# An mLSTM and two expert stages in one kernel: one transfer for q and k, three more staging buffers, all products of w3 first, the causal mask by TensorE

## The chip, the cores and the metric

The kernel runs on one core of one Trainium2 chip. Time is device time in microseconds (us). Each kernel is executed several times and once more under the hardware profiler; the profiled execution gives the trace from which all rows here are taken.

## What is computed

```python
for t in range(S):                                   # mLSTM, B=4, H=8, S=768, D=40
    m_new = maximum(f[t] + m, i[t])
    C = exp(f[t] + m - m_new) * C + exp(i[t] - m_new) * outer(v[t], k[t])
    n = exp(f[t] + m - m_new) * n + exp(i[t] - m_new) * k[t]
    y[t] = sigmoid(o[t]) * (C @ q[t]) / maximum(abs(n . q[t]), 1.0)
    m = m_new
x = y as [3072 tokens, 320]
x = ((x @ w1) * (x @ w2)) @ w3 @ w_out               # stage A, width 1024
out = maximum(x @ u1, x @ u2, x @ u3) @ u_out        # stage C, width 768
```

The weights come as 64-bit floats, all else as 32-bit floats; the output is 32-bit.

## The kernel before, in words

**Units.** The mLSTM is done in chunks of L = 87 time steps of one batch row, for all 8 heads at once: 4 x 9 = 36 units. `prepare` loads a unit's q and k (tile raw, two transfers, one for each half of the heads), q again at the partitions of the state (qq) and k and v (kv). `decay` makes the factors between time steps (tile dd). For the first 9 units (`ND`) it does so with a product on TensorE (L597) followed by exp on ScalarE (L600); later units load the exponents from a table d_na in DRAM, which four writes (L458) put there. In both cases GpSimd then zeroes what lies above the diagonal (`affine_select`, L615). `visit(v)` runs the score products of unit v (L675) and the output and state products of unit v-1 (L684). `rest` carries the state over (L720), divides (L732 to L735), multiplies by the gate (L740, GpSimd) and copies 64 columns to the tile's end (L743, GpSimd). `turn_x` transposes y (L750); `x_parts` splits it into a rounded part xh and its remainder xl.

**Blocks.** The two expert stages run over 8 blocks of 384 tokens. An A step (`a_step`) makes 128 columns of x @ w1 and x @ w2, in 16 products of 384 columns (L789 to L794); a `b_step` multiplies their product by w3 @ w_out (L899 to L903). `c_step` and `d_step` (L918) do the same for stage C. The order is A0 A1 C0 C1 A2 A3 and so on; visits stand at fixed steps (`USTEPS`), and from step `RIDE` on a visit is put into the middle of a step, where it can carry along the transposes of the unit before.

**Weights.** `granule` loads 512 columns of 64-bit weights (512 KB) into a staging buffer and turns them into 32-bit floats in place or into a target: ScalarE (L987), a shift on VectorE (L996) or its equal on ScalarE (L993), and VectorE (L1004). `parts` and `rem` split the result (L1014, L1017, L1029, L1036). There are three staging buffers stg and one, sx, that is there until the stage C weights come. `fold(ft)` decodes two granules of w3 and multiplies them with w_out at full 32-bit precision (L1054), as w3 @ w_out is needed once: 8 folds, five in the visits 1 to 5 (`FOLDS`), three ahead of the `b_step` that needs them. The first fold also decodes the 5 granules of w_out.

**Order.** No instruction order is written by hand. Each operation is entered with its engine, an assumed duration and the tiles that it reads and writes; `Plan.run` gives each a latest start, adds a correction from the table `BIAS`, and simulates the engines, always issuing the ready operation of the lowest value. An operation with two engines goes to the one that is free. All loads and stores are issued from one queue, SP's. A tile of a ring waits for the tile that had the buffer before.

**Shared space.** The tiles y, og, ev and pr lie in one buffer, misc, over the tiles of the gate computation (ff, aug, gft and others). A gate operation holds each ring back until the gate tiles below it have been read, the four writes of L458 among the readers of gft. A tile "kv" has the unit's data in partitions 0 to 95 and an identity matrix (`eyes`) in partitions 87 to 126, loaded once for each of its 3 buffers (L513).

Of the kernel before, what the change touches and what calls it, by code (L numbers as in the profile page):

```python
# [8 lines left out]
F32 = mybir.dt.float32  # L9
# [13 lines left out]
TB = 384  # L23
NBLK = B * S // TB
# [6 lines left out]
PRE = 6  # L31
# [26 lines left out]
XT_NS = 200  # L58
BIAS = {
# [3 lines left out]
    "Awa": 1483620, "Awar": 210300, "Awb0": -305840, "Awb1": 295600, "Awc": 213380, "Awcr": 343750, "Awd": 126180,  # L63
# [14 lines left out]
    "Gqqb": 186930, "Gwa": -943910, "Gwar": 1016950, "Gwc": 269610, "Gwcr": 31530, "Gwd": 243890, "Gy0": -450790,  # L78
# [26 lines left out]
def pool(n):  # L105
    return 150 + 2.1 * n


class Plan:
# [11 lines left out]
    def op(self, eng, ns, fn, r=(), w=(), after=(), cols=0, port=0, early=None):  # L121
# [163 lines left out]
def mlstm_moe_kernel(  # L285
# [50 lines left out]
    made["one", 0] = y[:, NCH * L + 1:NCH * L + 33]  # L336
    slots_nm = [lw["r", 0].rearrange("p a b c -> p (a b c)")[:, 0:8 * LE],
# [3 lines left out]
    for pool_, tag, bufs, n in (  # L341
# [3 lines left out]
        (tmp, "sx", EX, 1024), (tmp, "w3", L_BUFS, 512), (tmp, "raw0", RAW0, 8 * L),  # L345
# [8 lines left out]
    shared = (("y", TB), ("og", DM), ("ev", TB), ("pr", TB))  # L354
# [138 lines left out]
    P.op("G", 900, lambda: G.tensor_copy(na()[2][64:96], na()[1]), r=[("g", "msk")], w=[("hl", 1, 0)])  # L493
# [6 lines left out]
    new(("pt", 0), [128, NCH, 32], F32, "ac2")  # L500
# [11 lines left out]
    for i, t in enumerate(slots["kv"]):  # L512
        dma(71, lambda t=t: SP.dma_start(out=view(t, [128, 8, 81], F32)[L:R, :, 0:40], in_=eyes), w=[("kvb", i)])  # L513
# [4 lines left out]
    for c in range(SIGN):  # L518
        dma(318, lambda c=c: SP.dma_start(out=sg0[0:LP, c], in_=og[0, c]), w=[("sg", (0, c))])
# [57 lines left out]
    def decay(q):  # L577
# [5 lines left out]
        if q < ND:  # L583
# [9 lines left out]
            P.op(("V", "G"), (dve(8 * LE), 1400), (lambda: masked(V), lambda: masked(G)), r=[("hl", 1), ("one", 0)],  # L593
                 w=[("nm", q)], port=1)
# [673 lines left out]
```

## Time and profile before

| | us |
|---|---|
| median of 3 runs | 684.59 (682.53 to 685.3) |
| the profiled execution, its own time | 684.24 |
| its span, first to last instruction | 682.5 |
| TensorE busy in the span | 651.5 (95%) |
| VectorE, ScalarE, GpSimd busy | 372.9, 289.3, 248.0 |

PE is TensorE, PEld its weight loads, DVE VectorE, ACT ScalarE, POOL GpSimd, SPq the queue from which transfers are issued. L and a number is a line of the kernel. The time outside the span, 684.24 - 682.5 = 1.74 us, is launch and end.

### The profile page before, as it was taken

How to read it: one execution, taken by the hardware profiler on the slowest of the kernel's cores; microseconds unless marked ns; L12 is line 12 of the kernel's file. 1: busy time of each engine (PE TensorE's matmuls, PEld its weight loads, DVE VectorE, ACT ScalarE, POOL GpSimd, SP SyncE). 2: the span in 40 equal slices, each digit the busy share in tenths (PEclk: the TensorE clock that was granted, in tenths of full speed). 3: DMA queues.
4: the chain of work that ended last, by engine and by line, in shares of the span. 5: the costliest groups of instructions: out<-in, count | busy, mean ns of one | idle time of the engine just before them, and what ended most of it. 6: DMA issues, size and time to landing. Idle time of an engine off the chain costs nothing.

```text
span 682.5 us, 15124 instructions
## 1 busy us (share of the span) xinstructions
PE 651.5 (95%) x6199; PEld 618.1 (91%) x6199; DVE 372.9 (55%) x709; ACT 289.3 (42%) x546; POOL 248.0 (36%) x251
## 2 busy tenths in 40 slices
PE   3689989999999999999999999999999999999997
PEld 2456889899999999999999999999999989999997
DVE  7949985888853375443444474534344463323332
ACT  5726977656822435352522435432422322323111
POOL 4818972954521365232332354232132320000000
PEclk9999999999999999999999999999999999999999
DMA  8978769545520254211223162222023100000000
GB/s 211 265 219 248 229 190 273 167 131 165 162 80 30 64 158 127 65 48 29 61 69 79 48 175 75 68 69 67 2 78 82 40 30 1 1 1 1 1 30 29
DMA packets 33331, 65.97 MB, mean 97 GB/s; under 512 B 8974, under 2 KB 15502, under 8 KB 33262
## 3 DMA queue, kind: packets, MB, share of 16 engines
q1 hardware_dynamic: 33262, 65.01, 33.7%
q8 instruction: 48, 0.79, 0.5%
q14 instruction: 21, 0.17, 0.1%
HBM read 60.96 MB, written 4.03 MB: 95 GB/s over the span
## 4 chain that ended last, share of the span: by engine, by line
PE 84%; DVE 7%; ACT 3%; DMA 3%; issue 2%; POOL 1%; SPq 1%; DVEq 0%; POOLq 0%; ACTq 0%
PE wk L789 13%; PE wk L790 13%; PE wk L791 13%; PE acs L918 9%; PE wk L792 7%; PE wk L794 5%; PE acs L899 5%; PE acs L903 4%; PE wk L1054 3%; PE aq L684 3%; PE acs L901 3%; PE aq L675 2%; PE wk L804 1%; PE wk L750 1%; DVE w L1004 1%
## 5 line engine op out<-in xcount | busy, mean ns | idle before, releaser
L816 ACT CAST ph<-misc 128x384 fp32r<-128x384 f32 (+1 forms) x114 | 57.7, 507 | 144.7 <-PE acs L918 59.3
L866 DVE TENSOR_TENSOR misc<-misc,wk 128x384 f32<-128x384 f32 (+1 forms) x98 | 53.2, 545 | 113.9 <-PE wk L794 91.0
L642 POOL TENSOR_TENSOR pk<-qq,dd 63x696 f32<-63x696 f32 (+1 forms) x30 | 50.4, 1681 | 133.4 <-issue 117.6
L789 PE MATMUL wk<-xh,wch 128*128 128x384 f32 x288 | 97.1, 337 | 0.9 <-DVE misc L837 0.9
L791 PE MATMUL wk<-xl,wch 128*128 128x384 f32 x288 | 96.9, 337 | 0.0
L790 PE MATMUL wk<-xh,wcl 128*128 128x384 f32 x288 | 96.9, 336 | 0.0
L820 DVE TENSOR_TENSOR pl<-misc,ph 128x384 fp32r<-128x384 f32 (+1 forms) x91 | 60.5, 666 | 52.2 <-ACT ph L816 51.5
L789 PE MATMUL wk<-xh,wah 128*128 128x384 f32 x256 | 87.5, 342 | 0.0
L790 PE MATMUL wk<-xh,wal 128*128 128x384 f32 x256 | 86.3, 337 | 0.7 <-DVE wal L1017 0.7
L791 PE MATMUL wk<-xl,wah 128*128 128x384 f32 x256 | 86.1, 336 | 0.0
L837 DVE TENSOR_TENSOR misc<-misc,wk 128x384 f32<-128x384 f32 x64 | 35.1, 549 | 79.1 <-PE wk L794 46.4
L820 POOL TENSOR_TENSOR pl<-misc,ph 128x384 fp32r<-128x384 f32 (+1 forms) x23 | 24.5, 1067 | 146.6 <-ACT ph L816 108.6
L835 ACT COPY misc<-wk 128x384 f32<-128x384 f32 x64 | 30.5, 477 | 63.8 <-PE wk L804 35.2
L789 PEld LDWEIGHTS wk<-xh,wch 128*128 128x128 f32 x288 | 54.1, 188 | 1.2 <-DVE misc L837 1.2
L791 PEld LDWEIGHTS wk<-xl,wch 128*128 128x128 f32 x288 | 54.0, 188 | 0.0
L790 PEld LDWEIGHTS wk<-xh,wcl 128*128 128x128 f32 x288 | 54.0, 188 | 0.0
L608 POOL TENSOR_TENSOR dd<-am,dd 127x696 f32<-127x696 f32 (+2 forms) x27 | 39.0, 1448 | 38.0 <-DMA dd<-d_na 37.7
L918 PE MATMUL acs<-wd,ph 128*128 128x320 f32 x288 | 51.6, 313 | 0.7 <-DVE misc L961 0.7
L790 PEld LDWEIGHTS wk<-xh,wal 128*128 128x128 f32 x256 | 48.2, 188 | 1.5 <-DVE wal L1017 1.3
L789 PEld LDWEIGHTS wk<-xh,wah 128*128 128x128 f32 x256 | 48.2, 188 | 0.6 <-DVE xl L771 0.3
L792 PE MATMUL wk<-xh,wcr 128*128 128x384 f32 x144 | 48.4, 336 | 0.0
L791 PEld LDWEIGHTS wk<-xl,wah 128*128 128x128 f32 x256 | 48.2, 188 | 0.0
(144 smaller groups left out, 1351.9 us busy)
## 6 DMA issues: line engine op xcount, KB each, us to landing
raw<-in_qk SPq DMA_DIRECT2D x72, 130.5 KB, 4.0
kv<-in_kv SPq DMA_DIRECT2D x36, 243.0 KB, 3.5
dd<-d_na SPq DMA_DIRECT2D x21, 348.0 KB, 5.0
stg<-in_w3t SPq DMA_DIRECT2D x13, 512.0 KB, 6.3
stg<-in_wc SPq DMA_DIRECT2D x9, 512.0 KB, 4.4
qq<-in_qs SPq DMA_DIRECT2D x32, 130.5 KB, 4.0
out<-misc SPq DMA_DIRECT2D x24, 160.0 KB, 1.9
misc<-in_og SPq DMA_DIRECT2D x31, 120.0 KB, 3.3
```

The costliest lines, as they stand in the source:

```text
L608: P.op("G", 1400, lambda: G.tensor_tensor(out=T("dd", q)[:r], in0=am[:r, c, h0:h0 + 8].unsqueeze(2).to_broadcast([r, 8, n]), in1=T("dd", q ...
L642: e.tensor_tensor(out=T("pk", q)[64:R, :, 0:n], in0=T("qq", q)[64:R, :, 0:n], in1=T("dd", q)[64:R], op=ALU.mult)
L789: PE.matmul(p, lhsT=h_[:, kt], rhs=xh[:, kt], start=kt == 0, stop=False)
L790: PE.matmul(p, lhsT=l_[:, kt], rhs=xh[:, kt], start=False, stop=False)
L791: PE.matmul(p, lhsT=h_[:, kt], rhs=xl[:, kt], start=False, stop=False)
L792: PE.matmul(p, lhsT=r_, rhs=xh[:, 2], start=False, stop=False)
L794: PE.matmul(p, lhsT=r_, rhs=xl[:, 2], start=False, stop=True)
L816: P.op("A", act(n), lambda sl=sl: A.copy(out=T("ph", key)[:, sl], in_=T(*src)[:, sl]), r=[src + part], w=[("ph", key) + part])
L820: e.tensor_tensor(out=T("pl", key)[:, sl], in0=T(*src)[:, sl], in1=T("ph", key)[:, sl].bitcast(F32), op=ALU.subtract)
L837: P.op("V", dve(TB), lambda: V.tensor_tensor(out=T(*sa), in0=T(*sa), in1=T(*ps[1]), op=ALU.mult), r=[ps[1]], w=[sa])
L866: P.op("V", dve(sl.stop - sl.start), lambda sl=sl: V.tensor_tensor(out=T(*sc)[:, sl], in0=T(*sc)[:, sl], in1=T(*ps)[:, sl], op=ALU.max), r ...
L918: PE.matmul(T(f"ac{m}", (k, 1)), lhsT=src[:, m * 128:m * 128 + 128], rhs=w[:, o:o + DM], start=first_, stop=last_,)
```

## The change

- A unit's q and k come in one transfer of 112 partitions (rows 40 to 63 and 104 to 111 are padding) in place of two of 48.
- The buffer sx goes. Three buffers, s2, are laid over the place of ev and pr in misc, and used until the fourth A step of block 0 (`NP0` = 3); the first three A steps put their results into tiles of their own, pr0. The ring of staging buffers is 6 long until then and 3 long after, where it was 4 and later 3.
- All 8 folds stand in the visits 1 to 4.
- For the first 9 units the causal mask is added by TensorE: the product of an identity (eye) and a tile (tri) with 0 and -1e30 goes into PSUM ahead of the product of L597. GpSimd's `affine_select` stays for the other 27 units.
- `eyes` is loaded into partitions 96 to 127 alone, which the load of kv doesn't touch.
- The product of L635 and that of L740 may go to GpSimd or VectorE, the copy of L743 to ScalarE or GpSimd.
- Visits are placed at other steps (in blocks 2 to 7 one to two steps earlier), and at steps without a visit no unit is kept back for a ride: its transposes run there by themselves.
- The assumed durations and the table of corrections are new; the blocks' sizes and order are written in another way and stay the same (8 of 384, A0 A1 C0 C1 ...).

```diff
-FOLDS = (1, 2, 3, 4, 5)
+FOLDS = (1,1,1,2,2,3,3,4)
+NP0 = 3
-EX = 1
+EX = 0
...
+    made["eye", 0] = y[:, 1024:1152]
+    made["tri", 0] = x[:, NCH * 128:NCH * 128 + 4 * LE].rearrange("p (a b) -> p a b", b=LE)
...
-        (tmp, "sx", EX, 1024), (tmp, "w3", L_BUFS, 512), (tmp, "raw0", RAW0, 8 * L),
+        (tmp, "sx", EX, 1024), (tmp, "w3", L_BUFS, 512), (tmp, "raw0", RAW0, 8 * L), (tmp, "pr0", NP0, TB),
...
+    o = where["ev"][0]
+    slots["s2"] = [misc[:, o + i:o + i + 1024] for i in range(0, where["pr"][1] - o - 1023, 1024)]
+    where["s2"], over["s2"] = (o, where["pr"][1]), []
...
+    P.op("A", 300, f, r=[("cs", 0)], w=[("eye", 0)])
+    def f():
+        t = T("tri", 0).bitcast(F32)
+        G.memset(t, 0.0)
+        G.affine_select(out=T("tri", 0)[0:L], in_=t[0:L], pattern=[[0, 4], [1, LE]], compare_op=ALU.is_ge, fill=-1e30, base=0,
+                        channel_multiplier=-1)
...
-        dma(71, lambda t=t: SP.dma_start(out=view(t, [128, 8, 81], F32)[L:R, :, 0:40], in_=eyes), w=[("kvb", i)])
+        dma(71, lambda t=t: SP.dma_start(out=view(t, [128, 8, 81], F32)[LP:128, :, 0:40], in_=eyes), w=[("kvb", i)])
...
-                P.op("P", 190, lambda g=g, key=key: PE.matmul(
-                    T(*key), lhsT=T("hl", 0)[:, c], rhs=T("nm", q)[:, g * 4:g * 4 + 4], start=True, stop=True
-                ), cols=352, r=[("hl", 0), ("nm", q)], w=[key])
+                def f(g=g, key=key):
+                    PE.matmul(T(*key), lhsT=T("eye", 0), rhs=T("tri", 0), start=True, stop=False)
+                    PE.matmul(T(*key), lhsT=T("hl", 0)[:, c], rhs=T("nm", q)[:, g * 4:g * 4 + 4], start=False,
+                              stop=True)
+                P.op("P", 350, f, cols=704, r=[("hl", 0), ("nm", q), ("eye", 0), ("tri", 0)], w=[key])
...
-        for g in range(2):
-            dma(333, lambda g=g: SP.dma_start(out=T("raw", q)[g * 64:g * 64 + 48], in_=qk[b, c, g]), w=[("raw", q, g)])
+        dma(586, lambda: SP.dma_start(out=T("raw", q)[0:112], in_=qk[b, c]), w=[("raw", q)])
...
-        p = "sx" if not switch and i % (STG + EX) < EX else "stg"
+        ring = ["stg"] * STG + ["sx"] * (EX * (not switch)) + ["s2"] * (len(slots["s2"]) * (not s2_end))
+        p = ring[i % len(ring)]
...
+            if j == NP0:
+                s2_end.append(P.op("S", 0, lambda: None, after=[
+                    x for key, (_, _, acc) in P.state.items() if key[0] == "s2" for x in acc]))
+                gates_done["ev"] = gates_done["pr"] = s2_end[0]
...
-        keep = at >= RIDE and cur[0] <= NU and (kind == "C" or cols[0] >= (k + 1) * TB)
+        keep = at >= RIDE and cur[0] <= NU and at in visits and (kind == "C" or cols[0] >= OFF[k + 1])
```

## Rows read from the trace of the kernel before

**Rows 1.** Busy time of each engine in stretches of the span.

```profile
core 0: us, PE busy (x) PEld busy (x) DVE busy (x) ACT busy (x) POOL busy (x), PEclk, DMA share, GB/s
0.00:9.30 9.30, 0.00 (x0) 0.00 (x0) 6.32 (x7) 2.97 (x4) 4.42 (x14) 1.00 0.76 200
9.30:33.20 23.90, 15.36 (x197) 11.68 (x197) 21.62 (x30) 18.21 (x34) 15.91 (x13) 1.00 0.92 250
33.20:46.80 13.60, 12.35 (x37) 7.95 (x39) 5.91 (x15) 2.85 (x5) 4.14 (x5) 1.00 0.80 223
46.80:71.20 24.40, 21.88 (x383) 16.10 (x384) 22.16 (x43) 15.92 (x32) 17.87 (x16) 1.00 0.83 242
71.20:97.00 25.80, 23.00 (x326) 20.53 (x326) 23.10 (x41) 19.56 (x37) 21.04 (x19) 1.00 0.67 200
97.00:145.00 48.00, 48.00 (x324) 43.77 (x323) 35.99 (x55) 35.05 (x64) 29.26 (x25) 1.00 0.70 208
...
165.00:678.80 513.80, 511.81 (x4758) 499.71 (x4756) 238.86 (x494) 182.28 (x347) 143.28 (x151) 1.00 0.22 59
```

**Rows 2.** Timeline of PE: a fold half early and late, the first A group.

```profile
33.26 4.64 PE L1054 MATMUL wk<-wof,w 128*128 128x320 f32 x8 [0.66 <-DVE w L1004]
...
66.48 2.32 PE L1054 MATMUL wk<-wof,w 128*128 128x320 f32 x8
...
71.24 0.34 PE L789 MATMUL wk<-xh,wah 128*128 128x384 f32 x1
71.42 0.34 PE L790 MATMUL wk<-xh,wal 128*128 128x384 f32 x1
```

**Rows 3.** Timeline of PE at the sixth fold.

```profile
118.12 4.58 PE L1054 MATMUL wk<-wof,w 128*128 128x320 f32 x16
122.29 0.58 PE L789 MATMUL wk<-xh,wah 128*128 128x384 f32 x1
122.70 0.33 PE L790 MATMUL wk<-xh,wal 128*128 128x384 f32 x1
122.88 0.34 PE L791 MATMUL wk<-xl,wah 128*128 128x384 f32 x1
```

**Rows 4.** DMA from 0 to 71.2 us: packets, and the queue's share.

```profile
DMA packets 7538, 16.78 MB, mean 236 GB/s; under 512 B 2398, under 2 KB 3166, under 8 KB 7530
## 3 DMA queue, kind: packets, MB, share of 16 engines
q1 hardware_dynamic: 7530, 16.68, 83.7%
```

**Rows 5.** What SP's queue waited for, 20 to 71.2 us: total, times, longest.

```profile
SPq L982 <- DVE w L1004: 7.0, 4, 2.6
SPq L982 <- DVE wof L1004: 5.6, 4, 2.5
SPq L536 <- DMA kv<-in_eyes: 5.1, 1, 5.1
```

**Rows 6.** Timeline of SP's queue around the writes of d_na.

```profile
40.96 0.31 SPq L536 DMA_DIRECT2D kv<-in_kv  x1
41.32 0.42 SPq L625 DMA_DIRECT2D raw<-in_qk  x1
41.84 0.85 SPq L982 DMA_DIRECT2D stg<-in_w3t  x2
42.73 1.52 SPq L458 DMA_DIRECT2D d_na<-misc  x4
```

**Rows 7.** The page's DMA issues: KB each, median us from issue to landing.

```profile
raw<-in_qk SPq DMA_DIRECT2D x72, 130.5 KB, 4.0
kv<-in_kv SPq DMA_DIRECT2D x36, 243.0 KB, 3.5
dd<-d_na SPq DMA_DIRECT2D x21, 348.0 KB, 5.0
stg<-in_w3t SPq DMA_DIRECT2D x13, 512.0 KB, 6.3
```

**Rows 8.** Groups by line and shape, 0 to 97 us: busy us, mean ns.

```profile
L615 POOL TENSOR_SCALAR_AFFINE_SELECT dd<-dd 87x696 f32<-87x696 f32 x9 | 11.3, 1258 | 0.1
...
L1004 DVE SCALAR_TENSOR_TENSOR w<-stg 128x512 int32<-128x512 int32 x8 | 8.3, 1033 | 1.0 <-ACT stg L987 1.0
...
L597 PE MATMUL wk<-wcr,wch 128*128 128x352 f32 x10 | 5.0, 538 | 2.9 <-ACT dd L600 1.9 <-DVE wcr L587 1.0
...
L1065 DVE TENSOR_TENSOR wb<-wk,wb 128x256 fp32r<-128x256 f32 x5 | 2.1, 412 | 0.0
...
L996 DVE TENSOR_SCALAR stg<-stg 128x512 int32<-128x512 int32 x4 | 1.8, 443 | 4.5 <-DMA stg<-in_w3t 4.5
```

**Rows 9.** Timeline of PE: transposes in a ride and by themselves.

```profile
197.08 0.44 PE L750 MATMUL wk<-cs,misc 87*128 87x87 f32 x3
197.31 1.12 PE L918 MATMUL acs<-wd,ph 128*128 128x320 f32 x6
...
233.72 0.39 PE L750 MATMUL wk<-cs,misc 87*128 87x87 f32 x3
233.90 1.12 PE L918 MATMUL acs<-wd,ph 128*128 128x320 f32 x6
```

More of the change, by code (lines that the diff above doesn't have):

```diff
@@ L42 @@
 STG = 3
-EX = 1
+EX = 0
 L_BUFS = 4
 RCP = 8
-LAST = (NBLK - 1, 1, NC - 1)
 LATE = ("A", 1, 4)
 OC = 4 * L
+TB = max(SIZES)
+NBLK = len(SIZES)
+OFF = [sum(SIZES[:k_]) for k_ in range(NBLK + 1)]
+STEPS = [(x_[0], int(x_[1:]), j_) for x_ in ORDER.split() for j_ in range(8 if x_[0] == "A" else 6)]
+LAST = (NBLK - 1, 1, NC - 1)
+UNITS = [(t_ // S) * NCH + -(-(t_ % S) // L) for t_ in OFF[1:]]
+PRE = UNITS[0] + 1
 BUF = dict(x=3, y=3, og=3, ph=2, ev=3, raw=2, kv=3, qq=2, dd=3, pk=2)
@@ L166, in op @@
         name = tag + str(self.phase)
-        if self.phase == 0 and eng[0] in "DP":
+        if self.phase < 2:
             k = self.count[tag] = self.count.get(tag, -1) + 1
@@ L686, in f @@
             if turned:
-                turn_x(*turned)
+                turn_x(turned)
         r = [("raw", v)] * (v < NU) + [("pk", q), ("kv", q)] * (q >= 0)
         w, early, ns = list(toks), {}, 0
-        for has, part, cost in ((turned, None, XT_NS), (q >= 0, "o", 850), (v < NU, "s", 850), (pair, "p", 173)):
+        for has, part, cost in ((turned, None, XT_NS), (q >= 0, "o", 800), (v < NU, "s", 930), (pair, "p", 215)):
             if has:
@@ L765, in x_parts, with x_cols @@
+    def x_cols(key):
+        new(("xt", key), [128, 3, 128], F32, "wk")
+        P.op("P", 220, lambda: turn_x(key), cols=110, r=[("y", key[:2]), ("cs", 0)], w=[("xt", key)])
+        x_parts(key)
+    def x_parts(key):
+        b, c, t, end = key
+        t0 = b * S + c * L
+        cols[0] += end - t
+        while t < end:
+            k = max(x for x in range(NBLK) if OFF[x] <= t)
+            e = min(end, OFF[k + 1])
+            if t == OFF[k]:
                 xtiles((k, 0))
-            src = slice(t - c * L, e - c * L)
@@ L773, in x_parts @@
                 in1=T("xh", (k, 0))[:, :, to].bitcast(F32), op=ALU.subtract,
-            ), r=[("xt", (b, c)), ("xh", (k, 0), c)], w=[("xl", (k, 0), c)])
+            ), r=[("xt", key), ("xh", (k, 0), c)], w=[("xl", (k, 0), c)])
             t = e
-    def xtiles(key):
-        new(("xh", key), [128, 3, TB], F32R, "xh")
-        new(("xl", key), [128, 3, TB], F32R, "xl")
+    made_x = []
+    turns = [(0, 0), (1, 0)]
+    for k_ in range(NBLK):
+        turns += [(k_, 1), (k_ + 2, 0)]
+    turns = [x for x in turns if x[0] < NBLK]
@@ L782, in group @@
+    def xtiles(key):
+        while key not in made_x:
+            x = turns[len(made_x)]
+            made_x.append(x)
+            new(("xh", x), [128, 3, SIZES[x[0]]], F32R, "xh")
+            new(("xl", x), [128, 3, SIZES[x[0]]], F32R, "xl")
     def group(ps, key, wh, wl, wr, r, rest=True):
@@ L808, in thirds @@
     def thirds(key):
-        return [((m,), slice(m * 128, m * 128 + 128)) for m in range(3)] if key == LAST else [((), slice(0, TB))]
+        n = SIZES[key[0]]
+        return [((m,), slice(m * 128, m * 128 + 128)) for m in range(n // 128)] if key == LAST else [((), slice(0, n))]
     def phl(src, key):
-        new(("ph", key), [128, TB], F32R, "ph")
-        new(("pl", key), [128, TB], F32R, "pl")
+        n = SIZES[key[0]]
+        new(("ph", key), [128, n], F32R, "ph")
+        new(("pl", key), [128, n], F32R, "pl")
         for part, sl in thirds(key):
@@ L939, in split @@
         def split(kt, src, alt=False):
-            P.op("A", act(TB, not alt), lambda: A.copy(out=T("xh", key)[:, kt], in_=T(*src)),
+            P.op("A", act(n, not alt), lambda: A.copy(out=T("xh", key)[:, kt], in_=T(*src)),
                  r=[src], w=[("xh", key, kt)])
@@ L1013, in parts @@
         key, w = g
-        P.op("A", act(n), lambda: A.copy(out=h_(), in_=w()), r=[key], w=[tok + ("h",)], after=after)
+        P.op("A", wide(n), lambda: A.copy(out=h_(), in_=w()), r=[key], w=[tok + ("h",)], after=after)
         def f(e):
@@ L1108, in can, with some @@
     def can():
-        return pend and (pend[0][0] == 0 or ("xh", (0, 1)) in made)
+        if not pend:
+            return False
+        b, c, t, end = pend[0]
+        new_ = [(k, 0) for k, x in enumerate(OFF[:-1]) if t <= x < end and (k, 0) not in made_x]
+        i = len(made_x) - BUF["x"]
+        return not new_ or new_ == [turns[len(made_x)]] and (i < 0 or turns[i] in finished)
+    def some(k):
+        b, c, t, end = pend.pop(0)
+        x_cols((b, c, t, OFF[k + 1]))
+        pend.insert(0, (b, c, OFF[k + 1], end))
     def more(pair=None):
@@ L1126, in mlstm_moe_kernel @@
         while len(pend) > XLAG:
-            x_cols(*pend.pop(0))
+            x_cols(pend.pop(0))
     while pend:
-        x_cols(*pend.pop(0))
-    steps = []
-    for p in range(NBLK // 2):
-        for kind, nj in (("A", NA), ("C", NC)):
-            for k in (2 * p, 2 * p + 1):
-                steps += [(kind, k, j) for j in range(nj)]
-    nu = {}
-    for p in range(NBLK // 2):
-        span = [s for s in steps if s[1] // 2 == p]
-        for j in USTEPS:
-            nu[span[j]] = 1
+        x_cols(pend.pop(0))
+    at_a = [STEPS.index(("A", k, 0)) for k in range(NBLK)] + [len(STEPS)]
+    visits, v = {}, PRE
+    for k in range(1, NBLK):
+        a, n = at_a[k - 1], UNITS[k] + 1 - v
+        room = at_a[k] - a - VLAG[k > 1]
+        for i in range(n):
+            visits.setdefault(a + i * room // n, []).append(v + i)
+        v = UNITS[k] + 1
+    assert v == NU + 1 and all(len(x) == 1 for x in visits.values()), visits
+    finished = set()
     def last(src, key):
@@ L1159, in mlstm_moe_kernel @@
     gate = {}
-    for at, s in enumerate(steps):
+    for at, s in enumerate(STEPS):
         kind, k, j = s
@@ L1170, in mlstm_moe_kernel @@
             for q in range(3):
-                gate[q] = late_w(q) if q else [P.op("S", 0, lambda: None, w=[("hl", 0), ("hl", 1), ("one", 0)],
+                gate[q] = late_w(q) if q else [P.op("S", 0, lambda: None, w=[("hl", 0), ("hl", 1), ("one", 0), ("eye", 0), ("tri", 0)],
                                                          after=nm)]
@@ L1202, in _lay @@
     qs[:, :, 8:48] = qk[:, :, :, :, :, 0].transpose(0, 1, 3, 2, 4, 5)
-    rows = np.zeros((B, NCH, 2, 48, 4, 2 * L), f)
-    rows[:, :, :, 0:D] = qk.reshape(B, NCH, 2, D, 4, 2 * L)
+    rows = np.zeros((B, NCH, 112, 4, 2 * L), f)
+    for g in range(2):
+        rows[:, :, g * 64:g * 64 + D] = qk[:, :, g].reshape(B, NCH, D, 4, 2 * L)
     eye = np.eye(D, dtype=f)
@@ L1238, in _lay @@
         "kv": kvt,
[L1239 removed]
+        "eyes": np.repeat(np.concatenate([eye[LP - L:], eye[0:1] * 0])[:, None], H, 1),
         "og": og,
```

202 lines of the change are left out of this document (109 added, 93 removed), and 61 rows, old and new, of the table BIAS.

## The prediction

> **What bounds the kernel now.** I read the busy time by stretches first [rows 1]. From 97 us on TensorE has no gap to speak of: 48.0 of 48.0 us up to 145, and 511.8 of 513.8 from 165 to the last product. There only products that go away can shorten the kernel. Ahead of 97 us it is another kernel. TensorE is idle for all of the first 9.3 us, 8.5 of the next 23.9, 1.25 of the next 13.6, 2.5 of the next 24.4 and 2.8 of the 25.8 up to 97. VectorE is busy 21.6 of 23.9, 22.2 of 24.4 and 23.1 of 25.8 us in three of these stretches, and the 16 DMA engines have a share of 0.76 to 0.92 up to 71 us. In the third stretch, 33 to 47 us, the three engines that decode are slack (VectorE 5.9 of 13.6) while TensorE works off what it has.
>
> The timeline of TensorE comes next [rows 2]. The first A group starts at 71.24 us; what stands ahead of it are units and five folds. Half a fold took 4.64 us at 33 us and 2.32 at 66, though the granted clock reads 1.00, its level of 2.4 GHz, in both stretches [rows 1]. So the early products lose time beside the plain gaps, and the rows don't say why.
>
> The DMA views say what the early part waits for. 16.78 MB are moved up to 71.2 us, 236 GB/s at a share of 0.84 [rows 4], which would be 281 at a share of 1. SP's queue, one for all transfers, waits 12.6 us for staging buffers to be emptied (the two rows of L982 with VectorE) and once 5.1 us for `eyes` ahead of a load of kv [rows 5]. Behind that one wait stood, in order, a load of kv, one of q and k, two of w3 and the writes of d_na [rows 6]: the lull from 33 to 47 us.
>
> **The change, part by part.** *Folds.* Three of eight leave the gapless stretch. The one at 118.12 us holds TensorE until 122.29, and the product after it is followed after 0.41 us where 0.17 is usual [rows 3]: 4.17 + 0.24. The two others took 4.07 each by the same reading, so together 4.17 + 4.07 + 4.07 + 3 x 0.24 = 13.0 us. This is certain as long as the folds go into time that TensorE has ahead of the A steps.
>
> *What it costs to have them early.* I call d the delay of the first A group behind 71.24 us. Three resources set it.
> - DMA: six granules of 512 KB (3.15 MB) and the padding of q and k, 112 in place of 96 rows, 51 KB for some 7 units (0.36 MB), come on top of 16.78 MB: 20.3 MB. At 236 GB/s the added 3.5 MB take 14.8 us. At a share of 0.95, 267 GB/s, all of it takes 76.0 us, and d is 4.8.
> - TensorE: 13.0 us of folds and the masks' products have to go into 12.3 us of gaps between 9.3 and 71.2 us [rows 1], and into what the early products lose (2.3 us in the one half-fold of rows 2 alone). d is 0 if all of it is filled and some 17 if nothing is.
> - VectorE: six L1004 at 1.03 us, half of the six shifts (L996) at 0.44, three splits (L1065) at 0.41 [rows 8]: 6.2 + 1.3 + 1.2 = 8.7 us, against 12.2 idle from 9.3 to 71.2 [rows 1]. It sets no delay of its own as long as work is there whenever it is free.
>
> I take d = 6.5, nearer to the DMA's lower end. Of the waits of SP's queue those for staging buffers are the largest, and six buffers in place of four are just what they ask for; the wait for `eyes` ends too, as partitions 96 to 127 are not those of the load of kv. But the share stood at 0.92 for 24 us already, so it can't rise by much more than to 0.95.
>
> The Trainium skill would go lower: its page "DMA: Bandwidth & Descriptors", section Specifications, gives about 358 GB/s from HBM for one core, by which 20.3 MB land in 57 us and DMA sets no delay; the sum would then end at 670. The trace doesn't bear it out: the highest rate of a stretch is 250 GB/s [rows 1].
>
> *The mask.* GpSimd loses nine operations of 1.26 us [rows 8], each on the way from exp to the unit's products, and TensorE gets 18 products of 352 columns. One such product lasts 0.54 us in the mean; as A products of 0.34 us follow one another after 0.18 [rows 2], half of it is overlap, so 0.27 each and 4.9 us in all. About 14 fall ahead of the A steps and are in d's bounds; the rest (four, at 352 of 384 columns of an A product's 0.18) cost 0.6. Filling the tile tri and the identity is done once, in GpSimd's 4.9 idle us of the first 9.3.
>
> *The A steps up to 97 us.* TensorE idles 2.8 us there with VectorE and GpSimd at 23.1 and 21.0 of 25.8. Two or three masks less on GpSimd and three more products that have two engines to choose from should give back 1.5; the bounds are 0 and 2.8. Against it stands that the ring has three buffers from the fourth A step on, four before. Six granules are left then, and a step with its B step gives TensorE 24 products x 0.175 = 4.2 us of work, about what the decoding needs for one.
>
> *q and k in one transfer.* 304 KB should land in between 3.5 and 5.0 us, by the rows of 243 and 348 KB, where each half takes 4.0 [rows 7]: -0.5 to +1.0 us at the first unit, and hidden later, as it is issued a visit ahead. I take 0. Half of the 72 issues go from SP's queue; they cost nothing now.
>
> *Transposes by themselves.* In a ride they hold TensorE from 197.08 to 197.31, by themselves from 233.72 to 233.90 [rows 9]: no difference. Visits a step earlier change no amount of work. If y were late, TensorE would wait; the step between (2.8 us or more) covers it, so 0, with a bound of +1.
>
> The sum: 684.24 - 13.0 + 6.5 + 0.6 - 1.5 = 676.8 for the profiled execution, which lies 0.35 under the median. **I predict 677.0.**
>
> **The rivals.**
> 1. *The folds' early place is free.* DMA speeds up, the gaps are filled, d is 0 to 4.8. For it: 12.6 us of waits for staging buffers [rows 5], the lull. Against it: a share of 0.92 already. With d = 0 and all 2.8 us back: 684.2 - 13.0 + 0.6 - 2.8 = 669.0. The page's figure named above would bring this one.
> 2. *DMA takes back what the folds give.* The share stays, d = 14.8: 684.2 - 13.0 + 14.8 + 0.6 = 686.6, no change. For it: the share of 0.84, and VectorE at 90% in two of the three stretches. Against it: the queue's waits, which are for buffers and not for DMA. From d = 9.0 on, without the 1.5 us of the A steps, the change is under 0.5% (3.4 us, about what can be told from no change here).
> 3. *The new buffers open late.* They lie over the gate tiles, gft among them, and are held back until the four writes of d_na have read it. These leave at 42.73 us now [rows 6]. The ring goes round by count, so the fourth granule, of w_out, must go into the first new buffer, and the first product of w3 waits for it. If the writes stay there, that granule starts at about 44.3, lands 6.3 later [rows 7] and needs some 2 us of decoding: the first fold starts at 52 in place of 33.26, d is 19 or more, and the time is 684.2 - 13.0 + 19 + 0.6 = 691 or more, slower. It decides the sign from an opening at about 36 us on. Against it: gft has its last value at about 10 us, and the planner sees that six buffers wait for the writes and puts them ahead.
> 4. *The folds don't move*, since the order is the planner's. A fold's PSUM tile is one of a ring of three, and every later group waits for it, so a fold can't be put off for long. About 684.
>
> **How the numbers follow.** My forecast (d from 4.8 to 9.0) has 0.50, rival 1 0.19, rival 2 0.19, rival 3 0.10, rival 4 0.02. Faster by over 0.5% are the forecast and rival 1: 0.69. No change: 0.21. Slower: 0.10. The range leaves out rival 3 and the best end of rival 1, and goes from 669 to 687; that of the forecast alone, with 2.8 or nothing back in the A steps, is 674 to 681.
>
> **What would show it.** No L1054 after the first A group, and an A stretch without the three holes of 4 us (13.0). The first A group at 76 to 80 us; the DMA share up to there at 0.9 or more. Nine masks fewer on GpSimd, 36 records of L597's product. The wait for `eyes` gone, the writes of d_na ahead of 20 us. From 165 us on the same stretch as now, within 1 us. I am wrong if the first A group comes at 71 (rival 1) or after 81 (rival 2), or the first fold after 45 (rival 3), or if TensorE's gaps between the first A group and 120 us grow past 5 us, for which I have no term.

## The result, and the profile after

The changed kernel takes 687.5 us (median of 15, 684.0 to 693.3), the kernel before 683.7 (median of 15, 681.9 to 685.3): ratio 1.0062, 95% interval 1.0040 to 1.0084. It is slower by 0.6%, where I had predicted 677.0. The profiled execution took 690.33 us, 2.8 over its median; the changed kernel's executions spread over 9 us, those of the kernel before over 3.4.

The windows of the changed kernel, cut at its own landmarks (the first unit, the first fold, the first A group at 86.9 us), beside [rows 1]:

```profile
core 0: us, PE busy (x) PEld busy (x) DVE busy (x) ACT busy (x) POOL busy (x), PEclk, DMA share, GB/s
...
8.70:29.20 20.50, 11.18 (x117) 8.87 (x117) 16.26 (x20) 13.38 (x23) 7.50 (x7) 1.00 1.00 293
29.20:43.40 14.20, 12.07 (x190) 8.14 (x184) 10.59 (x23) 8.33 (x15) 7.61 (x5) 1.00 1.02 300
43.40:73.10 29.70, 28.84 (x209) 20.31 (x212) 23.02 (x44) 19.66 (x36) 12.96 (x10) 1.00 1.03 289
73.10:86.90 13.80, 11.02 (x179) 8.45 (x178) 11.10 (x23) 7.98 (x20) 5.97 (x6) 0.88 0.34 100
86.90:120.00 33.10, 30.25 (x372) 28.41 (x370) 25.63 (x44) 24.03 (x46) 27.73 (x21) 1.00 0.69 194
```

Two things are to be seen. The DMA share is 1.00 or more from 8.7 to 73.1 us, at 289 to 300 GB/s, where it was 0.80 to 0.92. And TensorE, from 43.4 to 73.1, has a gap of 0.86 us in 29.7. The lull of the kernel before is gone, and still the first A group comes late. The timeline of TensorE there, as [rows 2]:

```profile
86.91 0.34 PE L839 MATMUL wk<-xh,wah 128*128 128x384 f32 x1
87.08 0.34 PE L840 MATMUL wk<-xh,wal 128*128 128x384 f32 x1
```

86.91 in place of 71.24: d is 15.7 us. From there to the last product TensorE takes 597.7 us (before 607.5), 9.8 less. 15.7 - 9.8 is the 5.9 us by which the last product is later, and the profiled executions differ by 690.33 - 684.24 = 6.1 (the medians, 687.5 and 683.7, by 3.8).

The DMA view from 0 to 71.2 us, beside [rows 4], then SP's longest wait from 20 to 71.2 us, beside [rows 5], and the writes of d_na on SP, beside [rows 6]:

```profile
DMA packets 8142, 19.89 MB, mean 279 GB/s; under 512 B 2169, under 2 KB 2937, under 8 KB 8136
```

```profile
SPq L1054 <- DVE w L1076: 23.5, 10, 6.3
```

```profile
14.39 1.42 SPq L478 DMA_DIRECT2D d_na<-misc  x4
```

3.1 MB more than before by the same time, the wait for `eyes` gone, the writes of d_na at 14.39 us instead of 42.73. The wait for staging buffers, which the three new buffers should have cut, has grown from 12.6 us to 26.5 (23.5 and a row of 3.0 for w_out).

The clock in stretches of 2 us, and the fold half that runs in it:

```profile
72.00:74.00 2.00, 1.80 (x81) 1.39 (x80) 0.00 (x0) 1.52 (x4) 1.08 (x1) 1.00 1.01 260
74.00:76.00 2.00, 0.56 (x2) 0.30 (x2) 1.97 (x4) 0.87 (x2) 1.30 (x1) 1.00 0.44 117
76.00:78.00 2.00, 0.87 (x3) 0.90 (x4) 1.91 (x6) 1.56 (x3) 0.00 (x0) 0.79 0.19 16
78.00:80.00 2.00, 2.00 (x6) 1.20 (x5) 1.92 (x3) 0.46 (x1) 1.87 (x2) 0.50 0.84 326
```

```profile
69.92 2.35 PE L1126 MATMUL wk<-wof,w 128*128 128x320 f32 x8
...
77.13 0.62 PE L633 MATMUL wk<-wch,wcl 128*128 128x352 f32 x1 [1.51 <-DVE wb L1137]
77.56 0.49 PE L634 MATMUL wk<-wd,wch 128*128 128x352 f32 x1
77.85 3.66 PE L1126 MATMUL wk<-wof,w 128*128 128x320 f32 x8
```

After two waits between 73 and 77 us (1.27 and 1.51) the granted clock falls to 0.50, the level of 1.2 GHz. The half-fold at 77.85 us takes 3.66 us; the one at 69.92 took 2.35.

The prediction had taken transposes by themselves for free. The timeline of TensorE in a later block shows what stands behind them:

```profile
305.24 0.39 PE L791 MATMUL wk<-cs,misc 87*128 87x87 f32 x3
305.50 0.44 PE L839 MATMUL wk<-xh,wah 128*128 128x384 f32 x1
305.78 0.34 PE L840 MATMUL wk<-xh,wal 128*128 128x384 f32 x1
305.95 0.34 PE L841 MATMUL wk<-xl,wah 128*128 128x384 f32 x1
```

The first product after transposes holds TensorE for 0.28 us, the next for 0.17. That isn't new: behind the first A group there are 31 runs of transposes in either kernel. In the kernel before 13 of them are followed by a product of a B step (0.26 us in place of 0.17), 12 by one of a D step (0.23 in place of 0.15) and 5 by one of an A step; in the changed kernel 22 are followed by one of an A step. Of the stretch of 597.7 us the folds' 12.3 are gone and the masks' 0.6 have come; measured against the 9.8 that it is shorter, 12.3 - 0.6 - 9.8 = 1.9 us are left over. TensorE's gaps behind the first A group are alike in both kernels (5.7 and 5.6 us), so the 1.9 lie in products that hold TensorE longer; which of them is not shown.

### The profile page after: what moved, and what is told of

The parts are those of the page before. It is cut to its first block, busy times and chain, and to the rows that moved or that the text cites. A ratio compares the mean times of both kernels' runs of the same rounds, so it can differ in the third digit from the quotient of the medians.

```text
span 688.6 us, 15075 instructions
## 1 busy us (share of the span) xinstructions
PE 655.2 (95%) x6217; PEld 620.5 (90%) x6217; DVE 378.5 (55%) x710; ACT 295.6 (43%) x582; POOL 232.1 (34%) x209
## 4 chain that ended last, share of the span: by engine, by line
PE 76%; DMA 12%; DVE 5%; issue 2%; ACT 2%; POOL 2%; SPq 1%; DVEq 0%; ACTq 0%
PE wk L839 13%; PE wk L840 12%; PE wk L841 12%; PE acs L972 9%; PE wk L842 6%; PE wk L844 5%; PE acs L951 4%; PE acs L955 4%; PE aq L721 3%; PE acs L953 2%; PE aq L712 2%; DMA stg<-in_wa 2%; DMA dd<-d_na 2%; DMA kv<-in_kv 1%; DMA stg<-in_w3t 1%
## 5 line engine op out<-in xcount | busy, mean ns | idle before, releaser
L872 DVE TENSOR_TENSOR pl<-misc,ph 128x384 fp32r<-128x384 f32 (+1 forms) x79 | 50.1, 634 | 98.3 <-ACT ph L868 97.6
L839 PE MATMUL wk<-xh,wch 128*128 128x384 f32 x288 | 99.0, 344 | 0.8 <-DVE xl L812 0.8
L679 POOL TENSOR_TENSOR pk<-qq,dd 63x696 f32<-63x696 f32 (+1 forms) x26 | 44.2, 1701 | 160.2 <-issue 149.2
L868 ACT CAST ph<-misc 128x384 fp32r<-128x384 f32 (+1 forms) x111 | 55.9, 506 | 93.1 <-PE acs L972 44.0
L872 POOL TENSOR_TENSOR pl<-misc,ph 128x384 fp32r<-128x384 f32 (+1 forms) x32 | 33.5, 1051 | 129.6 <-ACT ph L868 79.3
L889 DVE TENSOR_TENSOR misc<-misc,wk 128x384 f32<-128x384 f32 x61 | 33.6, 551 | 65.7 <-PE wk L844 33.1
L915 ACT COPY misc<-wk 128x384 f32<-128x384 f32 x48 | 23.0, 479 | 101.0 <-PE wk L844 93.2
L887 ACT COPY misc<-wk 128x384 f32<-128x384 f32 x61 | 29.1, 477 | 50.7 <-PE wk L854 26.6
## 6 DMA issues: line engine op xcount, KB each, us to landing
raw<-in_qk SPq DMA_DIRECT2D x36, 304.5 KB, 4.0
qq<-in_qs SPq DMA_DIRECT2D x32, 130.5 KB, 4.4
```

The costliest lines, as they stand in the source:

```text
L679: e.tensor_tensor(out=T("pk", q)[64:R, :, 0:n], in0=T("qq", q)[64:R, :, 0:n], in1=T("dd", q)[64:R], op=ALU.mult)
L839: PE.matmul(p, lhsT=h_[:, kt], rhs=xh[:, kt], start=kt == 0, stop=False)
L868: P.op("A", act(n), lambda sl=sl: A.copy(out=T("ph", key)[:, sl], in_=T(*src)[:, sl]), r=[src + part], w=[("ph", key) + part])
L872: e.tensor_tensor(out=T("pl", key)[:, sl], in0=T(*src)[:, sl], in1=T("ph", key)[:, sl].bitcast(F32), op=ALU.subtract)
L889: P.op("V", dve(SIZES[k]), lambda: V.tensor_tensor(out=T(*sa), in0=T(*sa), in1=T(*ps[1]), op=ALU.mult), r=[ps[1]], w=[sa])
```

## The experiments

Most keep the order of every instruction: only what an operation does is edited, not what the planner knows of it. In the edits of FOLDS, of the rings and of the rule for rides the planner makes another order. "First A" is the start of the first A group in the profiled execution; it stands at 71.2 us in the kernel before and 86.9 in the changed one. Ratios are against the kernel before, run beside it. First A can differ by 1.6 us between two profiles of one order: the run a_ride below has the changed kernel's order up to 154 us, and its first A is 85.3.

**TensorE's share of the delay.** Fewer products in the changed kernel's last three folds:

```diff
-                for i in range(4):
+                for i in (range(4) if ft < 5 else (3 * q,)):
```

> The changed kernel in the same order of instructions, but the last three folds make 2 of their 8 products each (18 of 64 left out, so that part of w3 @ w_out is missing). A product is 0.52 us by the folds of the kernel before (4.17 us for 8), so 9.4 us of TensorE go. Theory T, TensorE itself is the limit from the first fold to the first A group: the time falls by 8 to 10 us, to about 678 from 687.5, and the first A group comes about 9 us earlier than 86.9. Theory S, the supply (DMA and decoding) sets the first A group: the gaps of TensorE grow by what the folds lose, the time stays within 2 us of 687.5.

688.8 us, ratio 1.0057 (1.0036 to 1.0078), first A 87.3. Nothing gained. Its windows show two reasons:

```profile
66.00:70.00 4.00, 2.75 (x22) 1.60 (x21) 3.68 (x4) 3.10 (x6) 2.94 (x2) 1.00 1.04 256
70.00:74.00 4.00, 1.23 (x70) 1.07 (x69) 4.00 (x4) 2.29 (x6) 3.31 (x3) 0.92 1.05 242
74.00:78.00 4.00, 1.28 (x24) 0.70 (x15) 3.06 (x8) 2.71 (x7) 1.29 (x1) 0.50 0.42 109
78.00:82.00 4.00, 3.98 (x11) 2.74 (x11) 3.83 (x8) 1.81 (x5) 2.97 (x3) 0.50 0.65 193
```

The loads run at a share of 1.04 until 74 us as before, and TensorE, which is now busy for 5.3 of the 12 us from 66 to 78, is granted half its clock when work comes. So TensorE alone is not the limit; how much the clock takes back isn't separated here.

The same in the kernel before, for its folds 1, 2 and 3 (condition `ft not in (1, 2, 3)`):

> The kernel before in the same order, but the folds 1, 2 and 3, which run ahead of its A steps, make 2 of 8 products each (18 left out). Theory T: the early place is not free in the kernel before either, the time falls by 8 to 10 us, to about 675. Theory G, that of the prediction, early folds lie in gaps of TensorE and are free: the time stays above 682.

685.4 us, ratio 1.0013 (1.0003 to 1.0024), first A 71.4. Three folds cut to a quarter give nothing here either. But here too the clock takes a part back (0.50 in every stretch of 2 us from 48 to 64), so this shows neither that the early folds of the kernel before are free nor how much room the gaps have.

Masks and rides in the changed kernel: without the mask's 18 products, and with the old rule for keeping a unit back for a ride.

```diff
-                    PE.matmul(T(*key), lhsT=T("eye", 0), rhs=T("tri", 0), start=True, stop=False)
...
-        keep = at >= RIDE and cur[0] <= NU and at in visits and (kind == "C" or cols[0] >= OFF[k + 1])
+        keep = at >= RIDE and cur[0] <= NU and (kind == "C" or cols[0] >= OFF[k + 1])
```

> The changed kernel in the same order, without the 18 products of the mask (the factors above the diagonal are left as they are for the first 9 units). By the trace of the changed kernel these products hold TensorE 5.1 us ahead of the first A group and 0.6 after it. Theory T: 5 to 6 us faster than the changed kernel, about 682. Theory S: within 1.5 us of 687.5.

688.1 us, ratio 1.0061 (1.0038 to 1.0085), first A 87.0: the masks' products cost no time that can be told from the changed kernel's own ratio, 1.0062 (1.0040 to 1.0084).

> The changed kernel with the rule of the kernel before for the transposes: a unit is kept back at every step for a ride with the next visit. Theory R, transposes by themselves cost one more slow first product (0.28 in place of 0.18 us) for each unit: 24 more of them in the changed kernel, 2.3 us, and the time falls to about 685. Rival: nothing falls in the gapless stretch (the transposes' own rows are the same), 687.5 within 1 us.

687.7 us, ratio 1.0055 (1.0034 to 1.0076), first A 85.3. This edit does change the order, from 154 us on. In its profile the part behind the first A group is 3.6 us shorter (594.1), but the median is that of the changed kernel; the gain in the one profile is not shown as a gain in time.

TensorE's waits for w3: the fold's products read w_out's tile in place of w3.

```diff
-                        T(*ps), lhsT=T(*w3)[:, i * 128:i * 128 + 128],
+                        T(*ps), lhsT=wof[:, i * 128:i * 128 + 128],
```

> The kernel after, every instruction in the same order; the fold's products read wof in place of w3, so that TensorE never waits for a granule of w3; loading and decoding of w3 stay. The product w3 @ w_out is left out, so the output is not the reference's. Theory Q (folds that wait for w3 at the head of TensorE's queue hold back the units' products behind them): first A group at 79 us or earlier in place of 86.9, 680 us or less. Rival (the units wait for something else: loads, VectorE, ScalarE): first A group at 84 us or later, 685 us or more.

689.8 us, ratio 1.0069 (1.0048 to 1.0090), first A 84.8. The folds' own waits at the head of TensorE's queue are worth 2.1 us of first A in the profile, little more than one profile differs from the next, and nothing in the time.

**Edits that give the planner another program.** The result tiles of the folds out of the shared ring (`"ac2"` in place of `"wk"`); FOLDS back to (1, 2, 3, 4, 5); the new FOLDS in the kernel before; one new staging buffer in place of three.

> The kernel after with one edit: the result tile of each of the eight early folds is the PSUM tile ac2, which nothing uses ahead of the first B step, in place of a tile of the ring wk, so that the units' decay products and transposes no longer stand behind folds in that ring. Nothing is left out. Theory R (the ring ties the units to the supply of w3, and so delays the visits and the first A group): the fourth to seventh visit come 8 us or more earlier (33 to 72 us now), the first A group at 76 to 80 us in place of 86.9, and 679 to 682 us. Rival S (the supply sets it: DMA and the decoding of 21 granules stand ahead of the units on SP, ScalarE and VectorE): first A group within 3 us of 86.9, 686 to 689 us.

> The kernel after with FOLDS as in the kernel before (one fold at each of the visits 1 to 5, three ahead of the B step that needs them); all other parts of the change stay. Nothing is left out. If the early folds alone are what delays the units, the first A group comes at 68 to 73 us, the three late folds take their 12.3 us back, and the time is 681 to 685 us, the time of the kernel before or a little less. If something else of the change delays the units (the six buffers, the transposes, the order of the planner), the first A group stays behind 80 us and the time is 690 us or more.

> The kernel before with one edit: FOLDS as in the kernel after, all eight folds at the visits 1 to 4. Nothing is left out. If the early folds delay the units, the first A group comes at 84 to 90 us in place of 71.2 and the time is 686 to 692 us: the loss of the change without its other parts. If the early folds are free as such (rival: another part of the change is to blame), the first A group comes by 76 us and the time is 674 to 680 us.

> The kernel after with one of the three new staging buffers in place of three: a ring of four up to the fourth A step, as in the kernel before. Nothing is left out. If the larger ring lets the loads of w3 run ahead of the units and crowd them out (of DMA and of the decoding engines), four buffers bring the visits forward, the first A group to 80 us or less, and the time to 683 us or less. If the larger ring feeds the folds, four buffers delay the last fold and the first A group by 3 us or more, and the time is 690 us or more. If the ring of PSUM tiles alone sets the pace, the time is within 2 us of 687.5.

| run | us | ratio, interval | first A |
|---|---|---|---|
| a_folds_ac | 712.3 | 1.0429 (1.0396 to 1.0463) | 103.5 |
| a_folds_back | 705.7 | 1.0328 (1.0306 to 1.0349) | 80.6 |
| b_folds_early | 704.6 | 1.0309 (1.0291 to 1.0328) | 97.1 |
| a_one_s2 | 705.1 | 1.0317 (1.0291 to 1.0344) | 93.7 |

a_folds_ac and b_folds_early miss every branch of what was expected. a_folds_back and a_one_s2 fall, by their numbers, into a branch that is open to the top (690 us or more), but the reasons given there don't account for a loss of this size. All lose 21 to 29 us on the kernel before, whatever the edit, even where FOLDS go back to what they were. In three of them all of the loss stands ahead of the first A group (22 to 32 us); in a_folds_back 9.3 us stand ahead of it and 10.2 behind. Each has a new order on every engine from 35 us on or earlier, with corrections that belong to another program. So they don't price the part that they edit; they show that the order can be worth more than any term of my sum. That the corrections are the cause is argued, not shown; in a_ride, with a new order from 154 us on, nothing was lost.

**The loads' share of the delay.** Again in the changed kernel's order; granule i is loaded in 16 of 128 partitions.

```diff
-        dma(n * 1.826, lambda: SP.dma_start(out=tl().rearrange("p a b -> p (a b)"), in_=src.bitcast(I32)),
+        m = 16 if 6 <= i < 21 else 128
+        dma(n * 1.826, lambda: SP.dma_start(out=tl()[0:m].rearrange("p a b -> p (a b)"), in_=src[0:m].bitcast(I32)),
```

> The kernel after, every instruction in the same order; of 15 of the 16 granules of w3 only 16 of 128 partitions are transferred (64 KB in place of 512 KB, 6.9 MB less), so the weights and the output are not the reference's. Decoding and products stay in full. Theory D (the DMA engines are the limit from 9 to 72 us: share 1.0, and loads of 5 to 9 us in the chain): 6.9 MB at 293 GB/s are 23 us; the first A group comes at 77 us or earlier in place of 86.9 and the time is 679 us or less. Rival O (the order of the engines and queues sets it, a granule's landing is hidden): first A group at 83 us or later, 684 us or more.

681.0 us, ratio 0.9956 (0.9942 to 0.9970), first A 80.5: 6.5 us less than the changed kernel, in first A and in the median. That lies between the two cases. Transfers do delay the first A group, but by 6.5 of the 15.7. What is next is in its windows:

```profile
30.00:50.00 20.00, 18.55 (x212) 12.90 (x213) 17.53 (x39) 13.28 (x25) 8.99 (x7) 1.00 0.41 118
50.00:71.00 21.00, 21.00 (x168) 14.88 (x168) 18.67 (x33) 14.31 (x28) 11.11 (x9) 1.00 0.79 228
71.00:90.00 19.00, 18.76 (x313) 16.37 (x310) 16.72 (x33) 13.50 (x30) 15.30 (x13) 1.00 0.50 142
39.02:80.46 41.44, 41.44 (x465) 30.61 (x466) 36.41 (x72) 28.49 (x57) 19.71 (x17) 1.00 0.56 162
```

TensorE is busy 21.0 of 21 us and then 18.8 of 19, and from 39.02 us to the first A group it has no gap at all; the chain that ended last consists of its products alone there. With the loads out of the way, its products end last.

The same relief in the kernel before, for 9 of the 10 early granules of w3:

> The kernel before, every instruction in the same order; of 9 of the 10 granules of w3 ahead of the A steps only 16 of 128 partitions are transferred (4.1 MB less), so the output is not the reference's. If transfers already limited the kernel before (share 0.84): 4.1 MB at 236 GB/s are 17 us, and the first A group comes 5 us or more earlier, 679 us or less. If they did not: first A group within 2 us of 71.2, 682 to 685 us.

681.0 us, ratio 0.9957 (0.9945 to 0.9970), first A 67.2. Between the two cases: transfers cost the kernel before 4.1 us of first A already, and 2.8 of the time.

Both reliefs, short loads of w3 and fewer products:

> The kernel after, every instruction in the same order, with both reliefs at once: 15 granules of w3 transferred in 16 of 128 partitions, and two of the eight products in each of the last three folds. The output is not the reference's. Theory L (two limits of equal size, TensorE's products and the transfers of w3; lifting one leaves the other): 9 us of products and 6.5 us of transfers go, first A group at 71 to 76 us in place of 86.9 (80.5 with the short transfers alone), 670 to 676 us. Rival C (the chain of the units' own operations is a third limit): first A group at 79 us or later, 679 us or more.

682.8 us, ratio 0.9983 (0.9958 to 1.0007), first A 83.2 in a profile that was 1.8 us over the median. Theory L falls: there is a third limit. TensorE is busy for only 2.2 of the 8 us from 66 to 74, and the clock follows:

```profile
68.00:70.00 2.00, 0.66 (x64) 0.53 (x56) 0.70 (x1) 0.93 (x2) 1.77 (x2) 1.00 0.87 236
70.00:72.00 2.00, 0.39 (x2) 0.30 (x2) 1.43 (x4) 1.41 (x4) 0.78 (x1) 0.98 0.16 50
72.00:74.00 2.00, 0.61 (x3) 0.35 (x2) 1.97 (x4) 1.56 (x3) 0.52 (x1) 0.50 0.00 0
...
82.00:84.00 2.00, 2.00 (x7) 2.00 (x8) 1.01 (x4) 1.01 (x3) 0.23 (x1) 0.50 0.56 130
```

The chain of this run has a load of `wa` from 61.27 to 68.99 us, with ScalarE standing at it. The same wait in the changed kernel, in ScalarE's timeline:

```profile
72.48 0.68 ACT L1059 ACTIVATE stg<-stg 128x512 f32<-128x512 f32 x1 [1.77 <-DMA stg<-in_wa]
73.05 0.69 ACT L1065 ACTIVATE stg<-stg 128x512 int32<-128x512 uint16 x1
73.64 0.36 ACT L809 CAST xh<-wk 128x261 fp32r<-128x261 f32 x1
```

xh of a unit (L809) and, behind it at 74.44, a fold's split (L1133, then L1137 on VectorE) wait for the granule; the units' products at 75.06 and 77.13 us waited for L1137. Two runs on it: the six granules of stage A's weights short (`21 <= i < 27`), alone and with the two other reliefs.

> The kernel after, every instruction in the same order; the six granules of stage A's weights that are loaded ahead of the first A group (two of war, four of wa) are transferred in 16 of 128 partitions (64 KB in place of 512 KB, 2.8 MB less in all), so the output is not the reference's. w3, decoding and products stay in full. Theory H (ScalarE stands at a granule of wa that takes 8.8 us to land, from 63.6 to 72.4 us, and behind it stand the parts of xt and of the folds, on which the units' products wait): first A group 3 to 7 us earlier (80 to 84 us), 681 to 684.5 us. Rival (TensorE's products and w3's transfers hold the end anyway): first A group within 2 us of 86.9, 686 us or more.

684.8 us, ratio 1.0005 (0.9989 to 1.0022), first A 85.5: 2.7 us less than the changed kernel in the median, but 1.4 in first A, where theory H asked for 3 to 7.

> The kernel after, every instruction in the same order, with all three reliefs: 15 granules of w3 and six of stage A's weights in 16 of 128 partitions, two of eight products in each of the last three folds. The output is not the reference's. Theory H: TensorE's idle time between 65 and 75 us in the run with the first two reliefs was ScalarE's wait for a granule of wa; it goes, and the first A group comes at 70 to 76 us in place of 83.2, 670 to 676 us. Rival (VectorE's own work, or another wait of the units): first A group at 79 us or later, 678 us or more.

681.5 us, ratio 0.9974 (0.9959 to 0.9988), first A 80.6. Theory H falls too: the three reliefs together give no more than the short loads of w3 alone. What is left, in its windows and in the chain that ended last:

```profile
30.00:50.00 20.00, 19.29 (x211) 13.15 (x212) 17.63 (x38) 13.40 (x24) 9.08 (x7) 1.00 0.43 118
50.00:70.00 20.00, 15.87 (x173) 10.81 (x175) 17.59 (x29) 13.21 (x26) 10.74 (x8) 0.96 0.45 126
70.00:80.00 10.00, 8.25 (x157) 6.17 (x149) 9.71 (x23) 7.14 (x16) 6.51 (x6) 0.73 0.18 46
```

```profile
63.55 1.67 DVE misc L1077
65.21 1.59 DVE w L1077
66.80 0.40 issue
67.20 1.58 DVE pk L672
68.78 0.79 DVE pk L746
69.58 0.92 DVE misc L1077
70.49 0.34 DVE xl L812
70.83 0.46 DVE wb L1138 x2
```

From 58.6 us to 80.2 nearly every piece of the chain is VectorE's: decoding (L1077) of w3 and of stage A's weights, and between the pieces of it the units' pk, xl and the folds' split. VectorE is busy 17.6 of 20 and 9.7 of 10 us.

**Parts of the change in the order of the kernel before.** `eyes` into partitions 96 to 127; then the mask by TensorE as well (two products for one at L597, no `affine_select` for the first nine units); q and k in one transfer; `eyes` with that.

```diff
-        dma(71, lambda t=t: SP.dma_start(out=view(t, [128, 8, 81], F32)[L:R, :, 0:40], in_=eyes), w=[("kvb", i)])
+        dma(71, lambda t=t: SP.dma_start(out=view(t, [128, 8, 81], F32)[LP:128, :, 0:40], in_=eyes), w=[("kvb", i)])
```

> The kernel before, every instruction in the same order, with one part of the change: eyes is loaded into partitions 96 to 127, so that a load of kv no longer waits for it. Nothing is left out. The wait of 5.1 us on SP goes. If the lull from 33 to 47 us came from that wait, the first A group comes 3 to 5 us earlier (66 to 68 us) and the time is 679 to 681 us. If something else is as late (rival), the first A group stays within 1.5 us of 71.2 and the time within 1.5 us of 683.7.

682.2 us, ratio 0.9971 (0.9960 to 0.9983), first A 69.4: 1.9 us, less than the wait of 5.1. It leaves nothing out, and its median is the lowest here of the kernels that leave nothing out, 0.3% below the kernel before.

> The kernel before, every instruction in the same order, with two parts of the change: eyes as above, and the causal mask of the first nine units by TensorE; their affine_select on GpSimd goes. Nothing is left out. Nine selects of 1.26 us stand on the way from exp to the visits: if they count, the first A group comes another 2 to 5 us earlier than with eyes alone, 675 to 679 us. If they are hidden (rival), within 1.5 us of the run with eyes alone.

684.8 us, ratio 1.0005 (0.9991 to 1.0019), first A 72.9. The mask by TensorE takes back what `eyes` gave. Two stretches of 2 us, with `eyes` alone and then with the mask as well:

```profile
22.00:24.00 2.00, 1.67 (x65) 1.58 (x66) 1.97 (x3) 1.99 (x4) 1.92 (x4) 1.00 1.02 364
24.00:26.00 2.00, 0.53 (x2) 0.08 (x1) 1.97 (x3) 1.85 (x4) 1.92 (x2) 1.00 1.00 263
```

```profile
22.00:24.00 2.00, 0.94 (x65) 0.89 (x66) 1.97 (x4) 1.99 (x4) 0.81 (x1) 0.94 0.80 203
24.00:26.00 2.00, 1.34 (x4) 0.89 (x4) 1.97 (x2) 1.27 (x3) 1.70 (x1) 0.50 1.04 302
```

TensorE is idle more from 20 to 24 us, and the clock is 0.50 from 24 to 36. Taking GpSimd's selects off the path brought nothing here; whether they were hidden, or the clock took back what they gave, this run doesn't separate.

> The kernel before, every instruction in the same order, with one part of the change: q and k of a unit in one transfer of 112 rows in place of two of 48. Nothing is left out. The prediction took 0 for it: within 1 us of the kernel before (684), first A group within 1 us of 71.2. If 36 issues fewer on SP's queue (0.42 us each) count: 682 us or less. If the padding or the larger transfer counts: 685.5 us or more.

683.9 us, ratio 1.0002 (0.9994 to 1.0011), first A 70.1: 0, as predicted.

> The kernel before, every instruction in the same order, with two parts of the change that need no new order: eyes in partitions 96 to 127, and q and k in one transfer. Nothing is left out. If they add up: the time of the run with eyes alone (682.2) and what the run with q and k alone shows against 684. If the issue of q and k is only seen once the wait for eyes has gone: 681 us or less.

683.4 us, ratio 0.9986 (0.9974 to 0.9998), first A 68.8: no more than `eyes` alone. Its interval overlaps that of `eyes` alone, so of that gain 0.1 to 0.3% is what the two runs bear out.

## Why the prediction was wrong

- **The failed step is d, the delay of the first A group: 6.5 forecast, 15.7 measured.** It came at 86.9 us, past the 81 that the prediction named as a sign of being wrong. I took the value "nearer to the DMA's lower end" and let TensorE's bounds, 0 to 17, stand as bounds. The DMA term was sized well: share 1.00 (I had 0.95), 19.9 MB by 71.2 us, 20.3 by about 73 (I had 76.0; the padding is 304.5 - 2 x 130.5 = 43.5 KB a unit by the trace, not 51, which moves d's lower end by some 0.2 us). But the first A group doesn't start when the loads are done.
- **The term that was sized wrong is TensorE's lower bound, "0 if all of it is filled".** Folds can fill only gaps behind the first fold. Of the 12.3 us of gaps 8.5 lie ahead of 33.2 us [rows 1], and the first fold starts at 33.26 [rows 2]; 3.7 us were left for 13.0 us of folds and the masks. In the changed kernel 9.3 us of gaps lie between 8.7 and 29.2 us, ahead of its first fold. From the first fold to the first A group, in the kernel before, the changed one, and the changed one with short loads of w3:

```profile
33.26:71.24 37.98, 34.26 (x418) 24.08 (x419) 28.05 (x57) 18.81 (x37) 21.99 (x21) 1.00 0.81 235
29.20:86.91 57.71, 51.94 (x568) 36.91 (x562) 44.71 (x89) 35.98 (x68) 26.55 (x21) 0.97 0.86 246
29.78:80.46 50.68, 49.23 (x565) 35.71 (x562) 45.35 (x90) 33.94 (x68) 26.39 (x21) 1.00 0.55 160
```

TensorE is busy 17.7 us longer in the changed kernel, 14.0 of them with folds; its first fold starts 4.1 us earlier, and its gaps grow from 3.7 to 5.8 us instead of being filled: 17.7 - 4.1 + 2.1 = 15.7. With short loads of w3 the gaps are filled, down to 1.5 us, and 15.0 - 3.5 - 2.3 = 9.2 us of delay remain. So with the gaps filled d was 9.2 in this order, not 0.
- **"VectorE sets no delay of its own as long as work is there whenever it is free"** did not hold under relief: with loads and products shortened, VectorE's chain ended last, at 80.2 us.
- So d is not set by one resource. In first A, fewer products on TensorE give nothing (with the clock at half), shorter loads of w3 6.5 us, of stage A's weights 1.4, all three 6.3. No relief brought the first A group ahead of 80.5 us: TensorE's products end there when the loads are short, and VectorE's chain ends there when products and the loads of stage A's weights go as well. Which part of the change made the order of units, folds and decoding on these two stays open, since the runs that change that order early lose 21 us or more whatever part they edit. VectorE's decoding wasn't relieved in a run.
- **The folds leave the gapless stretch: right.** No fold after the first A group, where 13.0 was the term: the three folds' 12.3 are gone. The last of their products starts at 83.8 us, ahead of the first A group, so rival 4 is out. The net behind the first A group is 9.8: the masks took their 0.6, and 1.9 us went to products that hold TensorE longer, for which my sum had nothing (the bound for transposes was +1).
- **Idle time of the A steps, -1.5:** nothing came back; TensorE idles 2.85 us between 86.9 and 120, as before.
- The sum with the measured terms: 676.8 + (15.7 - 6.5) + 1.9 + 1.5 + (13.0 - 12.3) = 690.1, against 690.33 in the profile. The 1.9 is what was left over, so that the sum comes out is no check of it.
- **The rivals.** Rival 2's time (686.6) is nearly the one measured, by luck: the share didn't stay at 0.84, it went to 1. Rival 3 is out (d_na written at 14.4 us). Rival 1's condition, DMA speeding up, was met, and its time was not. The q and k transfer at 0 and the masks at nearly 0 in this kernel were right. The page "DMA: Bandwidth & Descriptors" of the Trainium skill, Specifications, has about 358 GB/s as the limit from HBM for a core. These stretches, at a share of 1.00 to 1.03, moved 289 to 300 in the mean, and the 670 us worked out from 358 did not come.

## What to carry to other kernels

Work that is moved to an early stage fills only the gaps that come after its first operand has landed; count the gaps from there, not from the start. Here TensorE, DMA and VectorE were each busy for some 80 to 100% of the stretch from 43 to 73 us: three folds of 12.3 us brought 15.7 us of delay, and relieving one of the three showed the next. Where a planner's order is held by a table of corrections, price the parts of a change in a fixed order first: here four edits that made a new order early cost 21 us and more, and the one gain in a fixed order that leaves nothing out, 1.9 us (1.0 by the ratio where it was run with q and k beside it), was one wait taken away.

## What the runs showed of the hardware

- Taking products off TensorE can slow the ones that stay: with three folds cut to a quarter the granted clock was 0.50 from 74 to 86 us, where the full kernel had 0.50 from 78 to 80 and 0.79 and 0.86 beside it. In the kernel before, the same cut brought 0.50 from 48 to 64 us, where it had 1.00, and a time 0.13% longer.
- Sixteen DMA engines at a share of 1.0 moved 289 to 300 GB/s here in the mean of stretches of 14 to 30 us, with up to 364 in a stretch of 2 us; a load of w3 of 512 KB into stg took 7.4 us in the median from issue to landing up to 71.2 us, against 5.8 in the kernel before, at a share of 0.84.
- A product of 384 columns right after transposes held TensorE 0.28 us, the next ones 0.17.
